# One batch's v cast moved from GpSimd to ScalarE, its kv and nums placed later, and the last group's stores merged, in an attention and feed-forward kernel

## The chip, the cores and the metric

The kernel runs on one core of one Trainium2 chip. The metric is the device time of one execution in microseconds. Each time given is the median of a few executions. A core has five engines with instruction queues of their own, each worked off in order: TensorE (PE, with its weight loads as PEld), VectorE (DVE), ScalarE (ACT), GpSimd (POOL) and SyncE (SP, which here only issues DMA transfers).

## The reference

q, k and v have 8 batches, 8 heads, 576 positions and 64 features in float32. The attention is linear, with no softmax over positions:

```
phi(x) = concat(relu(x) * cos_w, relu(x) * sin_w)      # 64 -> 128 features, weights by position
kv  = sum over positions of phi(k)^T v                 # per batch and head, 128 x 64
z   = sum over positions of phi(k)
num = phi(q) kv ;  den = phi(q) z + 1e-6
x   = num / den                                        # heads side by side: 4608 tokens x 512
out = leaky_relu(x w_in, slope 0.01) w_out             # 512 -> 2048 -> 512, float32
```

## The kernel before, in words

**Groups.** The 4608 tokens go through the feed-forward part in 9 groups of 512. Groups 0 to 7 are the first 512 positions ("main") of the 8 batches. Group 8 holds the last 64 positions ("tail") of every batch.

**One batch's attention.** `k_main`/`k_tail` make phi(k) (tiles kpm and kpt, `phi_half`, line 230 on DVE), `v_main`/`v_tail` cast v from float32 (vst, vtl) to float16 (vmain, vtail; `copy`, line 236 on ACT and 238 on DVE or POOL), `kv_all` (line 292) does 36 matmuls into one PSUM tile and copies it out on ACT (line 296), z being a column of ones beside v. `q_prep` makes phi(q), SP transposes it by DMA (qpT, line 318), and `num` (line 342) multiplies 8 heads into the PSUM tile ps_num, of which there is one buffer, and divides on DVE (den, rden, xs: lines 358, 362, 363). There are four nums of 128 tokens to a batch. Then x is transposed, for batch 2 by PE and an ACT copy (`x_transpose`, line 407), for later ones by DMA.

**Product one** (x w_in) of a group is 16 units of four 128x512 matmuls (`f1_mm`, line 634), each followed, alone or in pairs, by leaky relu on ACT (line 650 for pairs, 660 for single units). For group 1 the units go in pairs into ps_h, of which there are two buffers, so pair n+2 waits until ACT has emptied pair n.

**Product two** (g w_out) splits both factors into 2x2 blocks and uses seven block products instead of eight (`p2`, line 692), with sums of blocks of w_out (`w2_sums`, lines 607 to 619: wb1, wb2, wb4 and one in place) and of g (`g_sums`, line 662), all on DVE. Results are copied out by ACT (`o_copy`, line 710) or added on by DVE (`o_add`, line 712) and stored by SP (`o_store`, line 717).

**The order.** From group 1 on, the order of the program is written out by hand: `put(pos, f, ...)` gives each piece a position, and all are issued in the order of positions. Product one of group 1 has its 16 units at positions 0, 2, ... 30, and product two of group 1 begins at 32.2. The attention of batch 2 (the third one, after 0 and 1) lies among these: its q, k and v steps, `kv_all` at 14 (between units 7 and 8, counted from 0), nums at 16, 19.5, 23 and 26.5, x transposes 3.5 later each. `w2_sums` and `g_sums` lie in the same stretch. Later groups run product one of group g beside product two of group g-1 and the attention of batch g+1.

**The end.** Product two of group 8 is `f2_last` (line 766): per block product and pair of 128 tokens its own copy or add, and stores of 64 tokens of one batch each by `o_store_tail` (line 721). The order of the block products is 1, 2, 6, 5, 7, 4, 3. The left columns of the lower half of the output (half_ = 1) are final after product 4, its right columns after 7; the left columns of half_ = 0 after 2, its right columns after 3. Before, all stores are issued after products 4 and 3, by SP: per pair two of 64x512 and four of 64x256, 12 in all.

Of the kernel before, what the change touches and what calls it, by code (L numbers as in the profile page):

```python
# [18 lines left out]
def kernel(  # L19
# [14 lines left out]
    nc = tc.nc  # L34
    B, H, S, D = q.shape
    F = 2 * D
    DM = H * D
    DFF = moe_w_in.shape[1]
    MAIN = J * P
    TAIL = S - MAIN  # L40
# [5 lines left out]
    N2 = MAIN // 2  # L46
    NG = B + 1
# [34 lines left out]
    st = {}  # L82
    ACT, DVE, POOL = nc.scalar, nc.vector, nc.gpsimd
# [634 lines left out]
            out_rows(g)[:, 2 * half_ : 2 * half_ + 2, :], st["ob", g, half_]  # L718
        )

    def o_store_tail(half_, pair, lo=0, hi=DM):
        i = 2 * half_ + pair
        for o in range(2):
            r0 = (2 * i + o) * S + MAIN
            nc.sync.dma_start(
                out[r0 : r0 + TAIL, lo:hi],
                st["ob", NG - 1, half_][o * TAIL : (o + 1) * TAIL, pair, lo:hi],
            )

    def f2_stream(g):  # L730
# [34 lines left out]

    def f2_last(g):

        evs = [(-0.1, False, o_tiles, (g,))]
        n_ = 0
        for n, bi, fresh in (  # L770
            (1, 0, True), (2, 1, True), (6, 0, False), (5, 2, True),
            (7, 0, False), (4, 0, False), (3, 2, False),
        ):
            for pair in range(2):
                for u in range(2):
                    evs.append((n_, True, p2, (g, n, pair, u, bi, fresh, False)))
                    n_ += 1
                end = n_ - 0.9
                if n == 1:
                    evs.append((end, False, o_copy, (g, 0, 0, bi, pair)))  # L780
                elif n == 2:
                    evs.append((end, False, o_add, (g, 0, 0, bi, pair)))
                    if pair == 1:
                        for u in range(2):
                            evs.append((end + 0.2 + u, False, g_sums, (g, u, 4)))
                elif n == 6:
                    evs.append((end, False, o_copy, (g, 0, 1, bi, pair)))
                elif n == 7:
                    evs.append((end, False, o_copy, (g, 1, 1, bi, pair)))
                    evs.append((end + 0.1, False, o_add, (g, 1, 1, 2, pair)))  # L790
                elif n == 4:
                    evs.append((end, False, o_copy, (g, 1, 0, bi, pair)))
                    evs.append((end + 0.1, False, o_store_tail, (1, pair)))
                    evs.append((end + 0.2, False, o_store_tail, (0, pair, 0, N2)))
                elif n == 3:
                    evs.append((end, False, o_add, (g, 0, 1, bi, pair)))
                    evs.append((end + 0.1, False, o_store_tail, (0, pair, N2, DM)))
        return evs

    bank1, bank2 = [], []  # L800
# [11 lines left out]
    def put(pos, f, *args):  # L812
        line.append((pos, len(line), f, args))
# [35 lines left out]
    for g in range(2, NG - 1):  # L849
        put_stream(f2_stream(g), lambda s: top[g + 1] + step * (LAG + s) + 1)  # L850
    put_stream(f2_last(NG - 1), lambda s: top[NG] + step * LAG + 2 + s)


# [6 lines left out]
    def k_steps(b, start, step, engs):  # L860
        put(start - 0.01, kp_tiles, b)
        for i in range(J):
            put(start + i * step, k_main, b, i, *engs)
        put(start + J * step, k_tail, b, *engs)

    def v_steps(b, start, step, eng):
        put(start, v_main, b, 0, 4, eng)
        put(start + step, v_main, b, 4, 8, eng)
        put(start + 2 * step, v_tail, b, eng)

    def q_steps(b, start, step, lag):
        for j in range(J):
            put(start + j * step, q_prep, b, j)
            put(start + j * step + lag, q_transpose_dma, b, j)
# [4 lines left out]
            put(start + j * step + lag, x_transpose_dma, b, j)  # L879

    for s, i, when in (
        (1, 0, 1), (1, 1, 2), (2, 0, 14), (2, 1, 16), (3, 0, 18), (3, 1, 20), (4, 0, 22), (4, 1, 24),
    ):
        put(when, w2_sums, i, s)

    q_steps(2, 1.5, 2.5, 1.5)
    k_steps(2, 3, 2, (DVE, DVE))
    v_steps(2, 8, 2, POOL)
    put(14, kv_all, 2)
    for j in range(J):  # L890
        put(16 + 3.5 * j, num, 2, j)
        put(19.5 + 3.5 * j, x_transpose, 2, j)

    load_steps(3, 14, 18, 10)
    q_steps(3, 36, 3, 2.5)
# [50 lines left out]
```

## Time and profile before

| | |
|---|---|
| median of 3 runs (lowest, highest) | 299.78 us (299.42, 300.0) |
| profiled execution: its own time | 299.76 us |
| its span, first to last instruction | 298.0 us |
| mean granted TensorE clock | 0.971 |
| PE busy / DVE / ACT / POOL | 278.4 / 168.8 / 130.7 / 34.4 us |
| HBM read / written | 36.70 / 9.44 MB |

Durations come from the profiled execution, whose span leaves 1.76 us of its time outside. In a timeline row, the first number is the start in us from the span's start, the second the length of the row's instructions taken together (xN of them), and a bracket at the end gives the idle time before them on that engine and what ended it. In a row of the chain of work that ended last, there are a start, a length, the engine, what it wrote and the line. PE's rows in a timeline overlap at their ends, since matmuls are pipelined and their ends modelled; the chain's rows do not overlap.

### The profile page before, as it was taken

To read this page: it belongs to the slowest core of one execution; us is meant where nothing else is said; L and a number is where in the kernel's file an instruction comes from. 1 tells how busy PE (TensorE), PEld (TensorE's weight loads), DVE (VectorE), ACT (ScalarE), POOL (GpSimd) and SP (SyncE) were. 2 spreads that over 40 slices of the span, in tenths; PEclk is the share of its full clock that TensorE was granted. 3 is DMA by queue.
4 is the path that set the end of the run, shared out by engine and by line. 5 is a ranking of instruction groups with operands and counts; after the bars stand their busy time and mean duration, and the time that the engine had idled before them with its cause. 6 is when DMAs were issued, how large, how long until landed. Compare 5 with 4: busy or idle time off the path is not lost.

```text
span 298.0 us, 5728 instructions
## 1 busy us (share of the span) xinstructions
PE 278.4 (93%) x2300; PEld 192.0 (64%) x2300; DVE 168.8 (57%) x390; ACT 130.7 (44%) x213; POOL 34.4 (12%) x43
## 2 busy tenths in 40 slices
PE   7689999949999899999999999999999999999990
PEld 3376555525676567766776777677776677676880
DVE  5761396963893695759375928674553733051520
ACT  4636547632635345334443444443454333444220
POOL 2055000190400030012003000300000000000000
PEclk9959999996999999999999999999999999999997
DMA  7999999999359998997999799797438311100314
GB/s 238 302 385 370 331 368 339 307 194 315 99 90 242 293 156 157 255 259 175 228 325 122 212 241 301 74 242 153 85 76 213 37 35 73 70 3 0 141 43 100
DMA packets 86923, 57.01 MB, mean 191 GB/s; under 512 B 56688, under 2 KB 81776, under 8 KB 86384
## 3 DMA queue, kind: packets, MB, share of 16 engines
q1 hardware_dynamic: 86896, 56.64, 76.6%
q8 instruction: 18, 0.29, 0.4%
q14 instruction: 9, 0.07, 0.1%
HBM read 36.70 MB, written 9.44 MB: 155 GB/s over the span
## 4 chain that ended last, share of the span: by engine, by line
PE 83%; DMA 5%; DVE 4%; issue 3%; SPq 2%; POOL 1%; ACT 0%; DVEq 0%; POOLq 0%; ACTq 0%
PE ps_h L634 34%; PE ps_o L692 31%; PE ps_h L425 5%; PE ps_o L441 3%; PE ps_num L347 3%; DMA kst<-in_k_dram 3%; PE ps_kv L277 2%; PE ps_h L692 2%; DMA vtl<-in_v_dram 2%; SPq L106 1%; DVE xs L363 1%; DVE xp L363 1%; DVE gs L244 1%; SPq L96 1%; PE ps_numh L382 1%
## 5 line engine op out<-in xcount | busy, mean ns | idle before, releaser
L634 PE MATMUL ps_h<-xT,w 128*128 128x512 f16 x512 | 131.1, 382 | 0.2 <-ACT xT L403 0.2
L660 ACT ACTIVATE g<-ps_h 128x512 f16<-128x512 f32 x112 | 66.9, 597 | 100.5 <-PE ps_h L634 89.7
L634 PEld LDWEIGHTS <-w 128*128 128x128 f16 x512 | 56.9, 114 | 31.0 <-issue 1.6
L692 PEld LDWEIGHTS <-g 128*128 128x128 f16 x640 | 61.5, 98 | 20.0
L692 PE MATMUL ps_o<-w,g 128*128 128x256 f16 x360 | 48.6, 273 | 0.0
L241 DVE TENSOR_TENSOR ob<-ps_o,ob 128x512 f32<-128x512 f32 (+1 forms) x24 | 15.8, 657 | 49.8 <-PE ps_o L692 31.8
L238 POOL CAST vmain<-vst 128x1024 f16<-128x1024 f32 (+1 forms) x13 | 19.2, 1499 | 138.1 <-DMA vst<-in_v_dram 115.0
L692 PE MATMUL ps_o<-wb,g 128*128 128x256 f16 x240 | 32.6, 273 | 0.0
L692 PEld LDWEIGHTS <-gs 128*128 128x128 f16 x256 | 24.7, 98 | 9.6
L358 DVE TENSOR_SCALAR den<-ps_num 128x8 f32<-128x8 f32 x28 | 4.6, 165 | 37.8 <-PE ps_num L347 37.6
L710 ACT COPY ob<-ps_o 128x512 f32<-128x512 f32 (+1 forms) x32 | 17.8, 557 | 13.8 <-PE ps_o L692 13.8
L363 DVE TENSOR_TENSOR xs<-ps_num,rden 128x512 f16<-128x512 f32 x28 | 19.4, 691 | 1.2 <-DVE rden L362 0.2
L230 DVE TENSOR_SCALAR qp<-qst,cos_t 128x512 f16<-128x512 f32 (+1 forms) x34 | 15.9, 466 | 4.6 <-DMA qst<-in_q_dram 4.6
L230 DVE TENSOR_SCALAR kpm<-kst,sin_t 128x512 f16<-128x512 f32 (+1 forms) x40 | 17.4, 449 | 0.7 <-DMA kst<-in_k_dram 0.7
L277 PEld LDWEIGHTS <-kpm 128*128 128x128 f16 x256 | 12.1, 104 | 7.6 <-DVE wb L244 3.3
L692 PE MATMUL ps_o<-w,gs 128*128 128x256 f16 x120 | 16.9, 272 | 0.0
L692 PE MATMUL ps_o<-wb,gs 128*128 128x256 f16 x120 | 16.2, 273 | 0.0
L230 DVE TENSOR_SCALAR qp<-qst,sin_t 128x512 f16<-128x512 f32 (+1 forms) x34 | 15.9, 467 | 0.0
L441 PE MATMUL ps_o<-w,g 128*128 128x512 f16 x64 | 15.3, 379 | 0.0
L425 PE MATMUL ps_h<-xT,w 128*128 128x512 f16 (+1 forms) x80 | 14.9, 343 | 0.0
L230 DVE TENSOR_SCALAR kpm<-kst,cos_t 128x512 f16<-128x512 f32 (+1 forms) x31 | 14.8, 476 | 0.1
L347 PEld LDWEIGHTS <-qpT 128*128 128x128 f16 (+1 forms) x256 | 11.2, 102 | 5.1 <-issue 3.7
(77 smaller groups left out, 242.7 us busy)
## 6 DMA issues: line engine op xcount, KB each, us to landing
qst<-in_q_dram SPq DMA_DIRECT2D x7, 1024.0 KB, 8.3
out_dram<-ob SPq DMA_DIRECT2D x14, 512.0 KB, 2.9
kst<-in_k_dram SPq DMA_DIRECT2D x6, 1024.0 KB, 7.2
vst<-in_v_dram SPq DMA_DIRECT2D x6, 1024.0 KB, 10.7
w1st<-in_moe_w_in_dram SPq DMA_DIRECT2D x8, 512.0 KB, 9.2
w2st<-in_moe_w_out_dram SPq DMA_DIRECT2D x4, 1024.0 KB, 12.5
kst<-in_k_dram SPq DMA_DIRECT2D x4, 512.0 KB, 10.7
vst<-in_v_dram SPq DMA_DIRECT2D x4, 512.0 KB, 9.6
```

The lines of the kernel that those rows point to most:

```text
L230: eng.tensor_scalar(out=o, in0=i, scalar1=0.0, scalar2=col, op0=ALU.max, op1=ALU.mult)
L238: eng.tensor_copy(o, i)
L241: nc.vector.tensor_tensor(out=o, in0=a, in1=b, op=ALU.add)
L277: nc.tensor.matmul(ps[:, (2 * cc + o) * NE : (2 * cc + o + 1) * NE], lhsT=kpm[:, h, j, :], rhs=vmain[:, h, j, :], start=(o == 0 and j == 0 ...
L347: nc.tensor.matmul(ps[lo:hi, h // 4, (h % 4) * NE : (h % 4 + 1) * NE], lhsT=qpT[:, h, lo:hi], rhs=kv[b][:, h, :],)
L363: nc.vector.tensor_tensor(out=xs, in0=ps[:, :, 0 : 4 * NE].rearrange("p a (b e) -> p a b e", e=NE)[:, :, :, 0:D], in1=rden.rearrange("p (a ...
L425: nc.tensor.matmul(ps[:, m % 2, lo:hi], lhsT=w1[m // 4][c // 2][:, c % 2, m % 4 : 512 : 4], rhs=xT[:, c, lo:hi], start=(c == 0 and lo == 0 ...
L441: nc.tensor.matmul(ps, lhsT=st["g", g][:, m, tt * P : (tt + 1) * P], rhs=w2[:, m, :], start=(m == 0), stop=(m == NFT - 1),)
L634: nc.tensor.matmul(ps, lhsT=w1[m // 4][c // 2][:, c % 2, m % 4 : 512 : 4], rhs=st["xT", g][:, c], start=(c == 0), stop=(c == NKC - 1),)
L660: nc.scalar.activation(st["gt", g, up + 1][:, :, u], ps, AF.Lrelu)
L692: nc.tensor.matmul(bank, lhsT=st[G2[n], g][:, m, pair * P : (pair + 1) * P], rhs=W2[n](m), start=(fresh and m == 0), stop=(m == NH - 1), s ...
L710: nc.scalar.copy(o_at(g, half_, col, pair), bank_of(bi, pair, pair is None))
```

## The change

Batch 2's v is cast by ACT instead of POOL, and starts half a position earlier; k steps start at 2 with a spacing of 2.5. `kv_all` moves from 14 to 16.5, so it comes after the first unit of the fifth pair, and the nums and transposes are spread over the units that follow. `w2_sums` are put elsewhere in DVE's order: wb1 ahead of everything, wb2 later, the others at the end of product one. In `f2_last`, `o_store_tail` stores both pairs of one output half in one transfer (64x2x256, two batches) wherever both are final, the columns done after products 2 and 7 are stored right then, and where `mixed` is given, ACT issues the transfer of the second half of the partitions. So there are 10 stores: SP issues 7, ACT 3.

```diff
-    def o_store_tail(half_, pair, lo=0, hi=DM):
-        i = 2 * half_ + pair
+    def o_store_tail(half_, pairs, col, engs):
+        o_src, cols = st["ob", NG - 1, half_], slice(col * N2, (col + 1) * N2)
+        tokens = out.rearrange("(h q o s) d -> h o s q d", h=2, q=2, o=2)
         for o in range(2):
-            r0 = (2 * i + o) * S + MAIN
-            nc.sync.dma_start(
-                out[r0 : r0 + TAIL, lo:hi],
-                st["ob", NG - 1, half_][o * TAIL : (o + 1) * TAIL, pair, lo:hi],
+            engs[o].dma_start(
+                tokens[half_, o, MAIN:S, pairs, cols],
+                o_src[o * TAIL : (o + 1) * TAIL, pairs, cols],
             )
...
+        both, sync2, mixed = slice(0, 2), (nc.sync, nc.sync), (nc.sync, ACT)
...
                     evs.append((end, False, o_add, (g, 0, 0, bi, pair)))
                     if pair == 1:
+                        evs.append((end + 0.1, False, o_store_tail, (0, both, 0, sync2)))
...
                     evs.append((end + 0.1, False, o_add, (g, 1, 1, 2, pair)))
+                    if pair == 1:
+                        evs.append((end + 0.2, False, o_store_tail, (1, both, 1, sync2)))
                 elif n == 4:
                     evs.append((end, False, o_copy, (g, 1, 0, bi, pair)))
-                    evs.append((end + 0.1, False, o_store_tail, (1, pair)))
-                    evs.append((end + 0.2, False, o_store_tail, (0, pair, 0, N2)))
+                    if pair == 1:
+                        evs.append((end + 0.1, False, o_store_tail, (1, both, 0, mixed)))
                 elif n == 3:
+                    one = slice(pair, pair + 1)
                     evs.append((end, False, o_add, (g, 0, 1, bi, pair)))
-                    evs.append((end + 0.1, False, o_store_tail, (0, pair, N2, DM)))
+                    evs.append((end + 0.1, False, o_store_tail, (0, one, 1, mixed)))
...
     for s, i, when in (
-        (1, 0, 1), (1, 1, 2), (2, 0, 14), (2, 1, 16), (3, 0, 18), (3, 1, 20), (4, 0, 22), (4, 1, 24),
+        (1, 0, -1), (1, 1, -1), (2, 0, 17), (2, 1, 21), (3, 0, 28), (3, 1, 31), (4, 0, 33), (4, 1, 34),
     ):
         put(when, w2_sums, i, s)
 
     q_steps(2, 1.5, 2.5, 1.5)
-    k_steps(2, 3, 2, (DVE, DVE))
-    v_steps(2, 8, 2, POOL)
-    put(14, kv_all, 2)
+    k_steps(2, 2, 2.5, (DVE, DVE))
+    v_steps(2, 7.5, 2, ACT)
+    put(16.5, kv_all, 2)
     for j in range(J):
-        put(16 + 3.5 * j, num, 2, j)
-        put(19.5 + 3.5 * j, x_transpose, 2, j)
+        put(18.5 + 3 * j, num, 2, j)
+        put(21.4 + 3 * j, x_transpose, 2, j)
```

In the changed program's order of instructions, ACT casts vmain (two instructions of 128x1024) between the second and the third leaky relu of group 1, and vtail (two of 64x256) between the third and the fourth. PE does unit 8, kv, unit 9, num 0, unit 10, transpose 0, num 1, units 11 and 12, transpose 1, num 2, unit 13, transpose 2, num 3, units 14 and 15, transpose 3. SP's order is the same as before up to the last stores.

## Prediction

> **What bounds the kernel now.** I read the page first: the chain of work that ended last (part 4) names PE for most of the span, so only a stage in which PE waits or runs slowly, or the ends of the span, can give time back.
>
> ```profile
> PE 83%; DMA 5%; DVE 4%; issue 3%; SPq 2%; POOL 1%; ACT 0%; DVEq 0%; POOLq 0%; ACTq 0%
> ```
>
> Then PE's waits between 56 and 81 us, where the change's first part lies (engine, line, what it waited for, us in total, times, longest), and the windows of that stretch (start:end, length, busy time of PE, PEld, DVE, ACT, POOL, then the granted PE clock, DMA share, GB/s):
>
> ```profile
> PE ps_kv L277 <- POOL vmain L238: 3.0, 1, 3.0
> PE ps_kv L284 <- POOL vtail L238: 1.2, 1, 1.2
> ```
>
> ```profile
> 58.00:60.00 2.00, 2.00 (x11) 1.02 (x9) 2.00 (x6) 1.42 (x2) 1.19 (x1) 1.00 1.62 287
> 60.00:62.00 2.00, 2.00 (x11) 1.04 (x10) 2.00 (x6) 1.20 (x2) 2.00 (x1) 1.00 1.09 123
> 62.00:64.00 2.00, 0.57 (x3) 0.19 (x2) 2.00 (x6) 1.02 (x1) 2.00 (x1) 1.00 1.07 231
> 64.00:66.00 2.00, 0.38 (x8) 0.38 (x8) 0.66 (x2) 0.00 (x0) 2.00 (x2) 0.89 0.78 192
> 66.00:68.00 2.00, 0.81 (x14) 0.70 (x12) 0.00 (x0) 0.00 (x0) 1.29 (x3) 0.50 1.01 311
> ...
> 70.00:72.00 2.00, 2.00 (x13) 1.00 (x12) 0.43 (x3) 0.00 (x0) 0.00 (x0) 0.50 1.09 350
> 72.00:74.00 2.00, 2.00 (x19) 1.10 (x18) 2.00 (x4) 1.12 (x2) 0.00 (x0) 0.90 1.15 286
> ```
>
> PE waits 4.2 us for batch 2's v cast, and its clock is at half from about 65.6 (0.89 on average in 64 to 66) to 72.4 (0.90 in 72 to 74). POOL's timeline says why the cast is late:
>
> ```profile
> 58.81 6.75 POOL L238 CAST vmain<-vst 128x1024 f16<-128x1024 f32 x1 [9.79 <-DMA vst<-in_v_dram]
> ```
>
> ```profile
> 66.50 0.85 POOL L238 CAST vtail<-vtl 64x256 f16<-64x256 f32 x2
> 78.65 2.48 POOL L238 CAST vmain<-vst 128x1024 f16<-128x1024 f32 x2 [11.30 <-DMA vst<-in_v_dram]
> ```
>
> v has landed at 58.81; the first cast then takes 6.75 us, while at 78.65 two take 2.48. DVE is busy without a gap until 64.66 (2.00 in three windows, then 0.66), and the cast ends 0.9 us after that: it hardly moves while DVE streams.
>
> At the end of the span, ACT's last copy, DVE's last adds, SP's last stores, and what follows:
>
> ```profile
> 288.31 0.37 ACT L710 COPY ob<-ps_h 128x256 f32<-128x256 f32 x1 [0.50 <-PE ps_h L692]
> ```
>
> ```profile
> 289.19 0.42 DVE L241 TENSOR_TENSOR ob<-ps_o,ob 128x256 f32<-128x256 f32 x1 [1.79 <-PE ps_o L692]
> 290.06 0.42 DVE L241 TENSOR_TENSOR ob<-ps_h,ob 128x256 f32<-128x256 f32 x1 [0.45 <-PE ps_h L692]
> ```
>
> ```profile
> L725 SPq DMA_DIRECT2D out_dram<-ob x12: 530/590/599, 287.8 to 294.8; - x12
> ...
> DMA to landing us min/median/max: 2.0/2.1/2.4
> ```
>
> ```profile
> SPq L941 <- DMA out_dram<-ob: 1.5, 1, 1.5
> ```
>
> The last result is ready at 290.48, but SP issues 12 stores one after another from 287.84 on, 0.63 us apart, the last at 294.8. It lands 2.1 later, at 296.9, and 1.1 us of closing work ends the span at 298.0.
>
> **Part one, product one of group 1.** PE's timeline has two short gaps at its start:
>
> ```profile
> 54.86 0.40 PE L399 MATMUL ps_xth<-ident,xp 128*128 128x128 f16 x4 [0.40 <-DVE xp L363]
> ...
> 55.94 6.63 PE L634 MATMUL ps_h<-xT,w 128*128 128x512 f16 x30 [0.25 <-ACT xT L403]
> ```
>
> In both orders PE has done units 0 to 7 at 62.6 (55.94 + 6.63). In the old one, product two begins at 80.38. The prices, from the chain (start, length) and ACT's groups:
>
> ```profile
> 76.19 1.73 PE ps_h L634 x8
> 77.91 0.26 PE ps_xt L411 x4
> 78.17 0.26 PE ps_num L347 x8
> ...
> 80.38 6.11 PE ps_o L692 x56
> ...
> 96.02 0.25 PE ps_kv L277 x8
> ...
> 97.26 0.86 PE ps_h L634 x4
> 98.12 0.27 PE ps_num L347 x8
> 98.42 0.18 DVE den L358
> ...
> 98.86 0.69 DVE xs L363
> ```
>
> ```profile
> L650 ACT ACTIVATE g<-ps_h 128x1024 f16<-128x1024 f32 x8 | 8.2, 1023 | 9.4 <-PE ps_h L634 9.4
> ...
> L236 ACT CAST vmain<-vst 128x1024 f16<-128x1024 f32 x1 | 1.0, 1044 | 0.4 <-DMA vst<-in_v_dram 0.4
> ```
>
> So at full clock: two units 1.73, a kv 1.24 (96.02 to 97.26), a num 0.26, a transpose 0.24, and from a num's end to its xs 1.16 (98.39 to 99.55). ACT has done this very cast in 1.04 us. The tail cast on ACT (64x256) isn't shown; between nothing and the 1.04 of the big one I take the 0.37 of the 128x256 copy at 288.31.
>
> ACT's queue now holds the casts between leaky relus 2 and 3, so they wait for v, and behind them waits relu 3, and behind that PE, which needs the ps_h buffer:
>
> ```profile
> 59.16 1.02 ACT L650 ACTIVATE g<-ps_h 128x1024 f16<-128x1024 f32 x1 [0.58 <-PE ps_h L634]
> 60.88 1.02 ACT L650 ACTIVATE g<-ps_h 128x1024 f16<-128x1024 f32 x1 [0.70 <-PE ps_h L634]
> ```
>
> ACT is free at about 60.1, after v's landing. Two casts at steps of 0.94 (ends overlap by 0.1) bring relu 3 from 60.88 to 61.96, ended 62.98; PE wants that buffer at 62.6 and loses 0.4. The tails run to 63.5, relu 4 to 64.5. PE: unit 8 to 63.84, kv to 65.08 (v complete at 63.5), unit 9 to 65.94; ACT has kv out at 65.72. Num 0 to 66.21, unit 10 to 67.07, wait for xs 0 to 67.42; transpose and num 1 (0.66 after a wait) to 68.08, units 11 and 12 to 69.81; transpose 1 and num 2 to 70.33, unit 13 to 71.20, wait for xs 2 to 71.54; transpose and num 3 to 72.20, units 14 and 15 to 73.93, transpose 3 to 74.15. Against 80.38: **6.2 us** less, with 1.1 of waits left. The longest gap is 0.4 us, so I take the clock to stay at 1.00.
>
> The fourth q transpose could bind num 3:
>
> ```profile
> 63.44 2.53 SPq L318 DMA_TRANSPOSE qpT<-qp x1
> ```
>
> ```profile
> DMA to landing us min/median/max: 6.6/6.6/6.6
> ```
>
> It lands at 70.0; num 3 wants it at 71.9. SP's order before it is unchanged and the loads behind it too, so batch 3's v still comes at about 78.6.
>
> The moved `w2_sums` give DVE the same instructions in another order. Its timeline has their price and the end of its stream behind product one:
>
> ```profile
> 84.93 1.28 DVE L244 TENSOR_TENSOR g<-g,gs 128x1024 f16<-128x1024 f16 x2
> ...
> 87.71 0.47 DVE L230 TENSOR_SCALAR kpm<-kst,cos_t 128x512 f16<-128x512 f32 x1
> ...
> 90.88 0.35 DVE L230 TENSOR_SCALAR kpt<-ktl,cos_t 128x256 f16<-128x256 f32 x1
> ```
>
> That is 0.6 a sum, 0.40 each for the eight kpm from 87.71 to 90.88. After xs 3 (73.3) DVE has seven sums in a row; gs2's second half, the fourth, is done at 75.7 and g12, the sixth, at 76.9. Product two (0.44 per four matmuls by the 6.11 for 56) wants them at 78.5 and 79.4: a cover of 2.5 us, so I cost the move at nothing.
>
> From 74.15 on, PE has the same sequence as before from 80.38. Its loads hang on DVE, ACT and POOL freeing buffers, which move with it, so I carry the 6.2 to the end.
>
> **Part two, the last stores.** Counted by the old clock: the four stores of columns done after products 2 and 7 go out while PE still works. After the last copy of product 4 (288.31 + 0.37) one store by SP and one by ACT, after each add of product 3 one by each. Each SP issue of 0.6 ends before the next is wanted (289.3, then 290.24 against 290.51). So the last two are issued at 290.51, land 2.1 to 2.4 later, 292.7, plus 1.1: 293.8 instead of 298.0, **4.2 us** less. An issue by ACT isn't shown; the nearest rows are SP's of this line, 0.53 to 0.60; the far bound is SP's 2.53 for a transpose, by which three on end start the last at 293.8, and the end is 298.9 (2.53, a landing 1.5 after it, 1.1), which is no gain left in this part. I take 0.6, the same kind of transfer.
>
> Sum: 299.76 - 6.2 - 4.2 = 289.3 by the profiled execution, which is 0.02 from the median of 299.78.
>
> **The rivals.**
> - *ACT's issues are slow*, 1.0 to 1.3 us: from 288.7 the third then starts 0.2 to 0.8 late and takes 0.4 to 0.7 longer, so 290.3. For it: nothing here shows ACT issuing. Chance 0.09.
> - *v of batch 3 starves on POOL in its turn.* It comes at 78.6, while DVE now streams from 73.3 to about 86.2 (seven sums, eight qp halves, the add and two sums of g21, eight kpm, two kpt), with wb4 in the pause after 80.2. Cast after that, in 2.48 and 0.85, it ends at 89.5. PE wants it at 96.02 - 6.2 = 89.8; if DVE's stream lasts 1 to 2 us longer, PE waits so long: 290.5. [...] Chance 0.08.
> - *PE's clock drops all the same*, as short waits add up: the 6.8 us at half clock cost up to 3.4, so 292.7. Against it: the gaps of 0.40 and 0.25 before 55.94 are followed by 1.00. Chance 0.08.
> - *Product one gains nothing*, another wait taking its place: 295.5. Chance 0.02.
> - *Slower than before:* v of batch 2 lands late, and ACT's in-order queue now holds relu 3 and PE behind it, where POOL would have held only kv. Every us past 60.1 is lost, plus 3.4 for the clock after a gap of 3 us. It decides beyond 60.1 + 10.4 - 3.4 = 67.1, against 58.8 in this trace; at 69.5 the time is 302. Chance 0.03.
> - *My waits are too long* (1.1 us of them): 288.4. Chance 0.08.
>
> **How the numbers follow.** The forecast has the remaining 0.62, its own range 288.7 to 290.1. The range reaches to the short-wait case below and the two of 1 to 2 us above: 288.0 to 291.3, 0.87 in all by these cases, and I shade that for what I have not thought of. About 0.2%, 0.6 us, is what a measurement can tell from no change: faster 0.96, same 0.01, slower 0.03.
>
> **What would show it.** Right: ACT casts of about 1.04 us from 60.1; no PE wait over 0.5 between 62 and 74; clock 1.00 there; product two beginning at about 74; SP's and ACT's last issues within 0.7 of the last add, the end 3.3 after it. Wrong: ACT waiting on DMA at 60, a POOL cast of several us at 78, kv of batch 3 waiting on it, or last issues on ACT well over 0.6.

## The result, and the profile after

| | before | after |
|---|---|---|
| median (lowest, highest), 4 runs each, us | 299.89 (299.42, 300.81) | 289.93 (289.79, 290.27) |
| ratio, with its 95% interval | | 0.9666 (0.9641 to 0.9691) |
| profiled execution: time, span, us | 299.76, 298.0 | 289.96, 288.2 |
| mean granted PE clock | 0.971 | 0.993 |

The forecast was 289.3 us. The two profiles can be laid side by side at three marks: S, where PE takes up product one of group 1 for good; F, where product two of group 1 begins; and A, where DVE's last add ends. These rows of after give S (from PE's timeline), F (from the chain) and A (from DVE's timeline: 284.25 + 0.42):

```profile
54.94 1.24 PE L634 MATMUL ps_h<-xT,w 128*128 128x512 f16 x5 [0.27 <-ACT xT L403]
```

```profile
73.47 6.11 PE ps_o L692 x56
```

```profile
284.25 0.42 DVE L241 TENSOR_TENSOR ob<-ps_h,ob 128x256 f32<-128x256 f32 x1 [0.45 <-PE ps_h L692]
```

| us | to S | S to F (product one of group 1) | F to A (everything between) | A to the end of the span |
|---|---|---|---|---|
| before | 55.94 | 24.44 | 210.10 | 7.52 |
| after | 54.94 | 18.53 | 211.20 | 3.53 |
| difference | -1.00 | -5.91 | +1.10 | -3.99 |
| forecast | 0 | -6.2 | 0 | -4.2 |

The 1.00 before S isn't the change's: S lay anywhere from 54.2 to 55.9 in the profiles of this study, in kernels with and without the change (54.24 in a second profile of the changed kernel). Part of it may be the clock's: in windows of 2 us from 14 to 22, it was 0.59, 0.50, 0.50 and 0.70 in before, and 0.66, 0.50, 0.99 and 1.00 in after. If it is either 1 or a half, that is 6.8 us at half clock in before and 3.4 in after. So not all of the rise in the mean clock is the change's either. The other three belong to the change.

**Product one.** ACT's timeline of after has the casts where the forecast put them, 1.0 earlier like everything, with relu 3 (L650) between them:

```profile
59.08 1.99 ACT L236 CAST vmain<-vst 128x1024 f16<-128x1024 f32 x2
60.97 1.02 ACT L650 ACTIVATE g<-ps_h 128x1024 f16<-128x1024 f32 x1
61.88 0.82 ACT L236 CAST vtail<-vtl 64x256 f16<-64x256 f32 x2
```

PE's waits between 55 and 80 us are now three short kinds in place of the 3.0 and 1.2 for POOL, and the clock column of the windows (the third number from the end) stays at 1.00:

```profile
PE ps_xt L411 <- DVE xs L363: 0.8, 2, 0.5
PE ps_h L634 <- ACT g L650: 0.5, 1, 0.5
PE ps_h L634 <- ACT xT L403: 0.3, 1, 0.3
```

```profile
64.00:66.00 2.00, 2.00 (x25) 1.19 (x21) 1.96 (x5) 1.39 (x2) 0.00 (x0) 1.00 0.74 170
66.00:68.00 2.00, 1.52 (x18) 0.92 (x17) 1.75 (x5) 0.82 (x2) 0.00 (x0) 1.00 0.89 267
...
70.00:72.00 2.00, 1.64 (x18) 0.86 (x17) 1.15 (x5) 1.47 (x3) 0.00 (x0) 1.00 1.12 342
```

**The middle.** Here is a wait that before did not have: PE stands 0.93 us for the transposed x of group 3, and the chain, which now runs through that transfer, agrees.

```profile
103.50 0.81 PE L634 MATMUL ps_h<-xT,w 128*128 128x512 f16 x3 [0.93 <-DMA xT<-xs]
```

```profile
98.58 4.78 DMA xT<-xs
```

**The end.** The stores of the last 64 positions by line and queue (shortest, median, longest issue in ns, then first and last start), and the time from issue to landing of the two that start last:

```profile
L725 SPq DMA_DIRECT2D out_dram<-ob x7: 489/597/684, 276.0 to 284.7; - x7
...
L725 ACTq DMA_DIRECT2D out_dram<-ob x3: 533/647/733, 282.9 to 284.7; - x3
```

```profile
DMA to landing us min/median/max: 2.0/2.1/2.2
```

SP and ACT start their last store at 284.7, at once behind the last add at 284.67; 2.2 later it has landed, and 1.3 us of closing work follow.

### The profile page after: what moved, and what is told of

The parts are those of the page before. It is cut to its first block, busy times and chain, and to the rows that moved or that the text cites. A ratio compares the mean times of both kernels' runs of the same rounds, so it can differ in the third digit from the quotient of the medians.

```text
span 288.2 us, 5725 instructions
## 1 busy us (share of the span) xinstructions
PE 275.6 (96%) x2300; PEld 190.0 (66%) x2300; DVE 170.4 (59%) x390; ACT 133.3 (46%) x217; POOL 26.1 (9%) x39
## 4 chain that ended last, share of the span: by engine, by line
PE 85%; DMA 4%; ACT 4%; DVE 3%; SPq 2%; issue 1%; DVEq 0%; ACTq 0%
PE ps_h L634 34%; PE ps_o L692 31%; PE ps_h L425 5%; PE ps_o L441 4%; PE ps_num L347 3%; DMA kst<-in_k_dram 3%; PE ps_h L692 2%; PE ps_kv L277 2%; DMA xT<-xs 2%; ACT g L650 1%; SPq L106 1%; DVE xs L363 1%; PE ps_numh L382 1%; PE ps_kvh L277 1%; SPq L96 1%
## 5 line engine op out<-in xcount | busy, mean ns | idle before, releaser
L634 PE MATMUL ps_h<-xT,w 128*128 128x512 f16 x512 | 129.8, 379 | 1.7 <-DMA xT<-xs 0.9
L238 POOL CAST vmain<-vst 128x1024 f16<-128x1024 f32 (+1 forms) x11 | 11.3, 1054 | 140.2 <-DMA vst<-in_v_dram 65.8
L230 DVE TENSOR_SCALAR qp<-qst,sin_t 128x512 f16<-128x512 f32 (+1 forms) x34 | 16.6, 487 | 0.0
L347 PEld LDWEIGHTS <-qpT 128*128 128x128 f16 (+1 forms) x256 | 10.9, 101 | 4.7 <-issue 3.1
L244 DVE TENSOR_TENSOR gs<-g,gs 128x1024 f16<-128x1024 f16 x16 | 11.0, 690 | 4.8 <-PE ps_o L692 2.3
```

Of the source, the lines that this page charges most:

```text
L230: eng.tensor_scalar(out=o, in0=i, scalar1=0.0, scalar2=col, op0=ALU.max, op1=ALU.mult)
L238: eng.tensor_copy(o, i)
L244: nc.vector.tensor_tensor(out=o, in0=a, in1=b, op=ALU.subtract)
L347: nc.tensor.matmul(ps[lo:hi, h // 4, (h % 4) * NE : (h % 4 + 1) * NE], lhsT=qpT[:, h, lo:hi], rhs=kv[b][:, h, :],)
L634: nc.tensor.matmul(ps, lhsT=w1[m // 4][c // 2][:, c % 2, m % 4 : 512 : 4], rhs=st["xT", g][:, c], start=(c == 0), stop=(c == NKC - 1),)
```

## The experiments

All kernels compute the whole reference; wb4_twice does two of the sums a second time. S, F, A as above, from each kernel's own profile. "Middle wait" is PE's longest wait behind F other than the 0.7 us for DVE at L347 that every kernel has; the last column is F to A without it.

| kernel | median us (lowest, highest) | ratio to before (95%) | S to F | F to A | A to end | middle wait, for | F to A less wait |
|---|---|---|---|---|---|---|---|
| before | 299.89 (299.42, 300.81) | | 24.44 | 210.10 | 7.52 | none | 210.10 |
| after | 289.93 (289.79, 290.27) | 0.9666 (0.9641, 0.9691) | 18.53 | 211.20 | 3.53 | 0.93, xT | 210.27 |
| stores_only | 293.57 (293.16, 294.38) | 0.9819 (0.9771, 0.9868) | 23.90 | 210.27 | 3.07 | none | 210.27 |
| product_only | 294.93 (294.09, 295.71) | 0.9861 (0.9811, 0.9912) | 19.00 | 211.43 | 7.85 | 1.16, xT | 210.27 |
| cast_only | 294.15 (293.07, 295.0) | 0.9824 (0.9764, 0.9883) | 18.99 | 210.58 | 7.88 | 0.3, ACT | 210.3 |
| place_only | 298.04 (295.65, 299.72) | 0.9971 (0.9941, 1.0002) | 23.71 | 211.10 | 7.51 | 0.8, xT | 210.3 |
| wb4_late | 289.99 (289.28, 290.5) | 0.9678 (0.9637, 0.9719) | 19.20 | 210.60 | 3.46 | 0.18, xT | 210.42 |
| stores_sp | 291.82 (290.49, 294.7) | 0.9746 (0.9694, 0.9797) | 19.44 | 211.14 | 4.92 | 0.7, xT | 210.4 |
| dve_short | 298.64 (297.3, 302.21) | 0.9978 (0.9942, 1.0014) | 24.07 | 210.11 | 7.52 | none | 210.11 |
| split_cast | 289.02 (288.59, 290.23) | 0.9653 (0.9611, 0.9695) | 18.85 | 210.93 | 3.43 | 0.7, ACT | 210.2 |
| after_again | 290.12 (289.64, 291.29) | 0.9712 (0.9687, 0.9738) | 18.59 | 211.53 | 3.44 | 1.26, xT | 210.27 |
| wb4_twice | 290.76 (290.05, 291.78) | 0.9731 (0.9704, 0.9759) | 18.57 | 212.30 | 3.50 | 2.02, xT | 210.28 |
| cast_stores | 290.06 (288.86, 291.62) | 0.9703 (0.9674, 0.9732) | 19.18 | 210.47 | 3.51 | 0.2, xT | 210.3 |
| tail_first | 289.65 (289.19, 290.81) | 0.9696 (0.967, 0.9721) | 18.64 | 210.28 | 3.47 | none | 210.28 |

The first four experiments ran on one chip (before there: 298.62), the next four on another (299.1), the last four on a third (298.65); times are compared within one of these, or by the ratios.

### The two parts taken apart

stores_only is before with the change's `o_store_tail` and `f2_last`. product_only is before with the change's positions and engine for batch 2's steps and `w2_sums`, and the old stores. cast_only and place_only split product_only once more:

```diff
 cast_only, against before
-    v_steps(2, 8, 2, POOL)
+    v_steps(2, 7.5, 2, ACT)
 place_only, against product_only
-    v_steps(2, 7.5, 2, ACT)
+    v_steps(2, 8, 2, POOL)
```

> The kernel before with the new stores alone. Theory (the two parts add up): the span ends 3.5 us after the last add instead of 7.5, so the time is about 295.9 us. Rival (the end is bound by the landing of the data, not by SP's issues): 298 us or more.

> The kernel before with the new v cast, positions and sums, but the old stores. Theory: product two of group 1 begins about 18.5 us after unit 0 instead of 24.4, and group 3 waits about 1 us for its transposed x, as in the changed kernel: 299.9 - 5.9 + 1.1, about 295 us. Rival (the wait for the transposed x is chance of one profile): about 294 us, without that wait.

> The kernel before with v of batch 2 cast by ACT and nothing else moved. Theory (the cast on POOL was the whole loss, the placement gives little): kv waits under 1 us for the tail cast, the clock stays at 1.00, product two of group 1 begins about 0.5 us later than in the changed kernel, and with wb4 where it was, no wait for group 3's transposed x: 294 us. Rival (kv and the nums have to lie later, or PE still waits): 296 to 298 us.

> The changed placement of kv, nums, k steps and sums, old stores, v cast by POOL. Theory (POOL starves while DVE streams): the first cast still takes 5 us or more, PE waits 3 us or more for v, 297.5 to 300.5 us depending on the clock. Rival (the placement alone hides the cast): about 295 us.

Measured: 293.57, 294.93, 294.15 and 298.04. The cast alone gains as much of product one as the cast with the new positions does: S to F is 18.99 with it, 19.00 with both, and 23.71 with the new positions alone. These are chain rows (F) of cast_only and then of product_only, started at S 55.75 and 55.62 (the rows end at 78.0, so F's lengths are cut there):

```profile
74.74 3.28 PE ps_o L692 x30
```

```profile
74.62 3.38 PE ps_o L692 x31
```

The interval of place_only takes in 1. Its cast took 4.0 us, not the 5 or more expected, for a reason that the next experiment shows. With the cast on ACT, no gain from the positions is clear in product one: S to F is 18.53 to 19.44 with them (after, after_again, wb4_twice, product_only, stores_sp) and 18.99 and 19.18 without (cast_only, cast_stores). In the middle they cost 0.7 to 1.3 us.

stores_only was expected at 295.9 and came 2.3 lower. Against before on its own chip (298.62) it gained 5.05, and its stores are worth 4.45 in the profiles (7.52 to 3.07). In its profile S was 1.6 earlier than in before's, and half clock lasted half as long, which the next experiment takes up; that these two make up the other 0.6 is not shown.

### Does the GpSimd cast wait for a pause of VectorE?

The forecast read from one row that POOL's cast hardly moves while DVE streams, and ends 0.9 behind the stream. dve_short keeps the cast on POOL and takes two sums of w_out out of the end of that stream; after it, DVE has nothing for some time:

```diff
-        (1, 0, 1), (1, 1, 2), (2, 0, 14), (2, 1, 16), (3, 0, 18), ...
+        (1, 0, 1), (1, 1, 2), (2, 0, 17), (2, 1, 17.5), (3, 0, 18), ...
```

> The kernel before with the two wb2 sums moved behind the first of the g sums, so that DVE's stream beside POOL's cast ends 1.2 us earlier. Theory (POOL gets on only once DVE pauses): the first cast ends 1.2 us earlier, after about 5.6 us, PE's first wait is about 1.9 us, and the time is 298.7 us if PE's clock falls all the same, 296 to 297 us if it holds. Rival (the cast is slow for a reason of its own): 6.75 us again, 299.9 us.

Three kernels have POOL's cast beside streams of DVE that end at other times than before's 64.66. stores_only, POOL's timeline and the last row of DVE's stream, which ends at 63.09:

```profile
58.88 5.12 POOL L238 CAST vmain<-vst 128x1024 f16<-128x1024 f32 x1 [9.96 <-DMA vst<-in_v_dram]
```

```profile
62.41 0.68 DVE L244 TENSOR_TENSOR wb<-w,wb 128x1024 f16<-128x1024 f16 x1
```

dve_short, the same two; its stream ends at 61.73:

```profile
58.65 3.98 POOL L238 CAST vmain<-vst 128x1024 f16<-128x1024 f32 x1 [9.90 <-DMA vst<-in_v_dram]
```

```profile
61.04 0.69 DVE L244 TENSOR_TENSOR gs<-g 128x1024 f16<-128x1024 f16 x1
```

place_only, POOL's cast and what DVE did at that time:

```profile
58.81 4.01 POOL L238 CAST vmain<-vst 128x1024 f16<-128x1024 f32 x1 [9.87 <-DMA vst<-in_v_dram]
```

```profile
61.24 0.68 DVE L244 TENSOR_TENSOR gs<-g 128x1024 f16<-128x1024 f16 x1
62.11 1.25 DVE L244 TENSOR_TENSOR gs<-g,gs 128x1024 f16<-128x1024 f16 x1 [0.20 <-ACT g L650]
63.28 1.52 DVE L244 TENSOR_TENSOR wb<-w,wb 128x1024 f16<-128x1024 f16 x1
```

The casts end at 64.00, 62.63 and 62.82, which is 0.91, 0.90 and 0.90 after DVE's first pause (before: 0.90). They begin at nearly one time, so it is the pause that sets the end here, not the landing of v or the cast's length. (The 5.6 us expected of dve_short went by before's stream; in dve_short S came 1.7 earlier, and the stream ended earlier with it.) In place_only DVE waited a mere 0.20 for g, and POOL's cast ended 0.90 after that wait began; then the roles are turned round: beside POOL's casts, two sums of 0.68 take 1.25 and 1.52.

dve_short's shorter stream brought PE's first wait down to 1.9, as this table of PE's waits shows, but not the time (298.64, ratio with 1 inside its interval):

```profile
PE ps_xt L411 <- DVE xs L363: 2.0, 2, 1.7
PE ps_kv L277 <- POOL vmain L238: 1.9, 1, 1.9
PE ps_kv L284 <- POOL vtail L238: 1.4, 1, 1.4
```

The two sums, now ahead of the first divide, made xs late by 1.7, and the clock fell all the same. Its windows (clock third from the end):

```profile
64.00:65.00 1.00, 0.53 (x10) 0.53 (x10) 0.00 (x0) 0.00 (x0) 0.40 (x1) 0.58 0.65 125
65.00:66.00 1.00, 1.00 (x21) 1.00 (x19) 0.00 (x0) 0.00 (x0) 0.00 (x0) 0.50 0.67 237
66.00:67.00 1.00, 1.00 (x9) 0.48 (x7) 0.00 (x0) 0.57 (x1) 0.00 (x0) 0.50 0.90 246
67.00:68.00 1.00, 1.00 (x12) 0.56 (x11) 0.00 (x0) 0.03 (x1) 0.00 (x0) 0.71 0.99 346
```

If the clock in a window is either 1 or a half, 0.58 means that half clock began at 64.16, and 0.71 that it ended at 67.58: 3.4 us of it. By the same reading it lasted 3.4 us in stores_only and 6.8 in before and in place_only, of which these are the first and the last windows:

```profile
64.00:65.00 1.00, 0.00 (x0) 0.00 (x0) 1.00 (x2) 0.00 (x0) 1.00 (x2) 0.76 0.82 112
...
71.00:72.00 1.00, 1.00 (x15) 0.69 (x14) 0.74 (x2) 0.16 (x1) 0.00 (x0) 0.83 1.09 346
```

Every kernel with the cast on POOL fell to half clock here in its profile, with waits of 3.2 to 4.4 us for kv in all; no kernel with the cast on ACT did in this stretch, with single waits up to 1.13: the clock is 1.00 in the windows of after, product_only, cast_only, wb4_late, stores_sp and split_cast, and in after_again, wb4_twice, cast_stores and tail_first a unit of four matmuls takes 1.02 or 1.03 there, against 1.91 at half clock (before, 69.11).

### What the issues by ScalarE are worth

```diff
 stores_sp, against after
-        ... mixed = slice(0, 2), (nc.sync, nc.sync), (nc.sync, ACT)
+        ... mixed = slice(0, 2), (nc.sync, nc.sync), (nc.sync, nc.sync)
```

> The changed kernel with all ten last stores issued by SP. Theory (issue time binds the end): six issues of 0.6 us in a row after product four, the last starts about 1.3 us later, 291.2 us. Rival (merging and the early stores did it all, ACT's share gives nothing): 289.9 us.

Measured: 291.82, and 4.92 from A to the end, 1.39 more than after. The stores of stores_sp from 280 us on:

```profile
L725 SPq DMA_DIRECT2D out_dram<-ob x8: 546/592/602, 282.4 to 287.0; - x8
```

Its last add ends at 285.48, its last store is issued from 287.0 on. So of the 4.0 us of this part about 1.4 come from ACT's sharing the issuing, and 2.6 from the merging and the earlier stores of finished columns. Issue time sets the end here.

### Where the middle gives 1.1 us back

By the table, the loss is the wait for the transposed x of group 3, and it stands in the kernels with the change's positions for `w2_sums` (after, after_again, product_only, place_only, stores_sp: 0.7 to 1.26), with at most 0.2 elsewhere. The suspected path: the late sums lie ahead of batch 3's phi(q) halves in DVE's queue; SP transposes these, and behind the transposes in SP's queue stand batch 4's loads; behind those, in SP's queue again, the transposes of x for group 3. wb4_late takes two sums out of DVE's queue ahead of phi(q), wb4_twice puts two more (repeated, with the same result) into it:

```diff
 against after
-        ..., (3, 0, 28), (3, 1, 31), (4, 0, 33), (4, 1, 34),
+ wb4_late   ..., (3, 0, 28), (3, 1, 31), (4, 0, 63), (4, 1, 64),
+ wb4_twice  ..., (3, 0, 28), (3, 1, 31), (4, 0, 33), (4, 0, 33.5), (4, 1, 34), (4, 1, 34.5),
```

> The changed kernel with the two wb4 sums put behind batch 3's k steps on DVE (positions 63 and 64 instead of 33 and 34). Theory (wb4 ahead of batch 3's q steps delays their transposes on SP, and all that SP issues behind them, up to group 3's transposed x): group 3's units no longer wait for it, 0.9 us less, 289.0 us. Rival (the loads of batch 4 collide with those transposes anyway): the wait stays, 289.9 us.

> The changed kernel with each wb4 sum done twice, so 1.2 us more of DVE ahead of batch 3's q steps (the result is the same). Theory (these sums delay SP's transposes and loads, and so group 3's transposed x): the k load of batch 4 is issued 13.2 us after product two of group 1 begins instead of 12.0, PE waits about 2 us for the transposed x, 291.1 us. Rival (that wait comes from elsewhere): the wait stays near 0.9 us, 289.9 us.

> The changed kernel unaltered, as the measure for the other three on the same chip: 289.9 us, product two of group 1 18.5 to 19.4 us after unit 1's matmuls begin, group 3 waiting 0.7 to 1.2 us for its transposed x.

SP's timeline has the load of batch 4's k at once behind the transposes of phi(q). First wb4_late, then after, then wb4_twice, where F was at 74.34, 73.47 and 73.20:

```profile
85.29 0.53 SPq L96 DMA_DIRECT2D kst<-in_k_dram  x1
```

```profile
82.70 2.62 SPq L318 DMA_TRANSPOSE qpT<-qp  x2
85.43 0.53 SPq L96 DMA_DIRECT2D kst<-in_k_dram  x1
```

```profile
87.08 0.53 SPq L96 DMA_DIRECT2D kst<-in_k_dram  x1
```

So it is issued 10.95, 11.96 and 13.88 behind F, and PE's wait is 0.18, 0.93 and, in wb4_twice,

```profile
104.32 1.89 PE L634 MATMUL ps_h<-xT,w 128*128 128x512 f16 x8 [2.02 <-DMA xT<-xs]
```

So none, two and four of these sums ahead of phi(q) give 0.18, 0.93 and 2.02. Since F itself came 0.9 later in wb4_late than in after, its wait alone would not prove the point. stores_sp settles it: it has after's order, and its F is at 74.34, as wb4_late's is. These are its load of k and its wait, then wb4_late's wait:

```profile
86.29 0.53 SPq L96 DMA_DIRECT2D kst<-in_k_dram  x1
```

```profile
PE ps_h L634 <- DMA xT<-xs: 0.7, 1, 0.7
```

```profile
103.61 1.89 PE L634 MATMUL ps_h<-xT,w 128*128 128x512 f16 x8 [0.18 <-DMA xT<-xs]
```

With one F, the load is issued 1.0 later and the wait is 0.5 longer: it is the sums' place that costs. In all fourteen profiles the wait is at most 0.2 where that load is issued up to 11.3 behind F, and 0.7 or more where it is issued 11.9 or more behind. The last column of the table closes the account: without this wait, F to A is 210.1 to 210.4 in every kernel. The last leg is read from the traces and was not tested by itself. The nums are not late: the first xs of group 3 begins 18.5 behind F in wb4_late, after and wb4_twice alike. SP issues its transpose 0.07, 0.55 and 2.9 after that xs is done, in the last two right behind the last load of v. By the rows of the four transposes of x, the last one starts 25.1, 25.1 and 28.5 behind F and takes 4.0, 4.8 and 2.5 to land, so it is there 29.1, 29.9 and 31.0 behind F. In wb4_twice SP's queue is late; in after the transpose starts as early as in wb4_late but is 0.8 longer under way, beside loads that were issued 1.0 later. wb4_twice is 0.64 slower than after_again on the same chip (its intervals overlap).

wb4_late as a whole was no faster (289.99). In its profile S to F is 0.67 longer than in after, most of it at the fourth num, which now waits for the q transpose that the forecast had 1.9 us clear:

```profile
71.96 0.43 PE L347 MATMUL ps_num<-kv,qpT 128*128 128x66 f16 x8 [0.46 <-DMA qpT<-qp]
```

stores_sp, whose order is after's up to the end, has 0.48 there, after none. So this transfer is nearly binding, in some executions and not in others.

### Versions that may be better

cast_stores leaves all positions as before and takes only the new stores and the cast on ACT. split_cast is wb4_late with the second half of vmain behind relu 3, so that relu 3 and PE are held up by one cast only; tail_first swaps that half with the tail, which kv wants earlier:

```diff
 cast_stores, against stores_only
-    v_steps(2, 8, 2, POOL)
+    v_steps(2, 7.5, 2, ACT)
 split_cast, against wb4_late
-    v_steps(2, 7.5, 2, ACT)
+    put(7.5, v_main, 2, 0, 4, ACT)
+    put(11.2, v_main, 2, 4, 8, ACT)
+    put(11.4, v_tail, 2, ACT)
 tail_first, against split_cast
-    put(11.2, v_main, 2, 4, 8, ACT)
-    put(11.4, v_tail, 2, ACT)
+    put(11.2, v_tail, 2, ACT)
+    put(11.4, v_main, 2, 4, 8, ACT)
```

> As wb4_late, and ACT's two big casts split: one before relu 3, one behind it, so that relu 3 frees its buffer 0.9 us earlier. Theory (relu 3 behind two casts cost PE 0.47 us): that wait goes and kv still finds v complete, 288.5 us. Rival (the wait moves to kv, which needs v by then): 289.0 us as wb4_late.

> The kernel before with v of batch 2 cast by ACT and the new stores; kv, nums, k steps and sums where they were. Theory (the placement gives back on the transposed x what it gains): as fast as the changed kernel, 289.7 us. Rival (the later kv and nums are worth their own): 291 us or more.

> As split_cast, but with the tail cast ahead of the second big cast, since kv's first heads need the tail and not that one. Theory: kv no longer waits 0.4 us, no wait for the transposed x, 288.6 us. Rival (the wait moves to the nums, whose division on DVE sets the pace): 289.0 us.

cast_stores took 290.06, after_again 290.12: the one line of the cast and the stores do all that the change does. split_cast took 289.02, 1.0 under wb4_late on the same chip, and tail_first 289.65, 0.5 under after_again on the same chip, both with overlapping intervals: neither is clearly better. Why moving the casts brings so little is seen in PE's waits between 55 and 80 us, of split_cast and of tail_first:

```profile
PE ps_xt L411 <- DVE xs L363: 1.2, 2, 0.9
PE ps_kv L284 <- ACT vtail L236: 0.4, 1, 0.4
```

```profile
PE ps_xt L411 <- DVE xs L363: 1.5, 2, 1.1
...
```

Once relu 3 and kv come sooner, PE waits longer for the first xs: the way from kv over num and DVE's divide to the transpose sets the pace, behind the sums in DVE's queue.

## Why the prediction was right, and where it was off

**Product one: right, 5.91 for 6.2.** The cause held in each step: this cast hardly moves on POOL while DVE streams (four kernels, 0.90 to 0.91 behind the pause; a later cast got in otherwise, see the rivals); ACT does it in 1.04 a piece; relu 3 follows at 60.97 (forecast 60.96 with the 1.0 taken off); the clock stays. The missing 0.3 is at one place. The forecast gave num 0 to xs 1.16 us, as for an idle DVE. DVE's timeline of after has a sum of g in the way:

```profile
65.00 0.68 DVE L241 TENSOR_TENSOR g<-g,g 128x1024 f16<-128x1024 f16 x1
65.60 0.16 DVE L358 TENSOR_SCALAR den<-ps_num 128x8 f32<-128x8 f32 x1
```

num 0 was done at about 65.27, den begins at 65.60. So PE's first transpose starts at 66.78, which is 0.36 later than the forecast's 67.42 less the 1.0 before S, and that 0.3 is carried to F.

**The stores: right, 3.99 for 4.2.** ACT's issues took 0.53 to 0.73 us against the 0.6 taken; the rival of slow issues is out. The closing work was 1.3 instead of 1.1.

**The step that failed: "I cost the move at nothing".** The cover of 2.5 us was worked out for the two products that read the sums, and they did come in time. But DVE's queue also held batch 3's phi(q) behind those sums, and on SP's queue everything behind its transposes. That cost a wait of 0.93 (1.26 in the second profile), which goes with the sums and doubles with them. The forecast named DVE's stream and its seven sums, but asked of them only who reads them, not who stands behind them. So 289.3 was 0.6 too low: 0.3 from the divide, 0.2 at the end, 1.1 in the middle, less the 1.0 by which S came earlier in the profile of after. That last term is luck: without it the forecast would have been 1.6 too low. On the third chip before took 298.65 and after_again 290.12, 8.5 apart instead of 10.0.

**The rivals.** *v of batch 3 starves on POOL* did not come about, though the two engines met. Here POOL's cast got in although DVE's rows show no pause, and it was DVE that was held up. So the forecast's reading, that the cast waits for the end of the stream, holds for batch 2's cast at 58.8 and not for this one; what decides which of the two engines is held up is not shown. POOL's timeline of after, then DVE's, where the second row is 0.48 elsewhere and the third's two sums 1.28:

```profile
78.03 2.32 POOL L238 CAST vmain<-vst 128x1024 f16<-128x1024 f32 x2 [28.80 <-DVE qp L230]
```

```profile
77.80 0.48 DVE L230 TENSOR_SCALAR qp<-qst,cos_t 128x512 f16<-128x512 f32 x1
78.19 1.27 DVE L230 TENSOR_SCALAR qp<-qst,sin_t 128x512 f16<-128x512 f32 x1
...
79.98 1.72 DVE L244 TENSOR_TENSOR g<-g,gs 128x1024 f16<-128x1024 f16 x2
```

Together 1.2 us, in and ahead of the very halves of phi(q) that SP waits for. *The clock drops all the same*: not in this stretch, in any kernel with the cast on ACT. *Product one gains nothing*: it gained 5.91. *v lands late*: ACT never waited for it, so the price of an ACT queue that stands behind a DMA was not tried. *Faster by 0.9 with shorter waits*: the waits came out as long as forecast.

**What stays open.** Why F to A less the wait is 210.10 in before and dve_short and 210.27 in most others; and why S varies by 1.7 us. The clock can be part of it, but not all: S is 55.94 and 54.94 in before and after, with 6.8 and 3.4 us at half clock ahead of it, and 54.24, 54.90 and 55.21 in after_again, stores_sp and tail_first, whose mean clocks are 1.000, 1.000 and 0.999. Nor is it shown why before's times spread from 297.8 to 302.3 in all its runs here and after's (with after_again) from 289.6 to 291.3. Half clock can be part of that too, but not all: before took 301.74 at a mean clock of 0.969 and 298.13 at 0.981, but also 302.25 at 0.982, and after_again took 289.64 and 291.29, both at 1.000.

## What to carry to other kernels

A row of 6.75 us for work that takes 1.04 elsewhere is a wait in disguise: compare its end with the end of another engine's stream, not with its own start. When a step is moved ahead in a queue, list everything that stands behind it in that queue and what other queues those feed, not only who reads its result. At the end of a kernel, count the store issues behind the last result and share them between two engines (worth 1.4 us of 290 here).

## What the runs showed of the hardware

- A cast on GpSimd of 128x1024 from float32 to float16 (1.0 us without such a neighbour, two in 2.02 at 104.21 in before) made hardly any headway beside a stream of VectorE of up to 5.85 us (it took 6.75 in before), and ended 0.90 to 0.91 us after VectorE's first pause began, even one of 0.20 us, in four kernels (before, stores_only, dve_short, place_only). A later cast, at 78.03 in after, got in without a pause in VectorE's rows. Where GpSimd was in, some of VectorE's instructions of 0.48 to 0.68 us took 1.25 to 1.52 (place_only, after).
- Half clock of TensorE lasted 3.4 or 6.8 us, in four kernels out of four with waits of 3.2 to 4.4 us in two pieces with matmuls between them (1.85 and 1.37 in dve_short were enough), and did not come after a single gap of 2.02 (wb4_twice, before 104.32: 1.00 on average from 74 to 285). Early in the span of after it came with gaps of 0.66, 0.48 and 1.34 that ended at 11.9, 12.8 and 14.9; after_again, the same program, had none (mean clock 1.000). What sets its start and its length is not shown.
- Issuing a store of 64 partitions took 0.49 to 0.68 us on SyncE and 0.53 to 0.73 on ScalarE (after), landing 2.0 to 2.2 in the last two. With all ten on SyncE, the span ended 4.92 us behind the last add instead of 3.53 (stores_sp): 1.4 us of 290.
